# The opening of a fused Mamba-2 and hard-swish kernel: C loaded by heads, and the state ahead of decoding

## The chip, the cores and the metric

The kernel runs on one core of a Trainium2 chip. The core has TensorE (PE in the profile, PEld for its loads of weights), VectorE (DVE), ScalarE (ACT), GpSimd (POOL) and SyncE (SP), which here only issues DMAs. Each engine takes its instructions in the order of the program and waits on semaphores for the others. DMAs are issued from a queue (SP's, or ACT's) and run on sixteen DMA engines. The metric is the time of one execution in microseconds (us); less is better.

## What is computed

The reference, cut to what matters. Inputs: x (4, 8, 768, 32), a (4, 8, 768), B and C (4, 8, 768, 16), w_in (256, 2048), w_out (2048, 256). x, a, B, C are float32, and the two weights come in float64.

```python
# state-space block, chunk by chunk of the sequence; H = 8 heads, N = 16, D = 32
log_a = np.log(np.clip(a, 1e-06, 1.0))
state = np.zeros((batch, H, N, D))
for c in range(nc):
    cum = np.cumsum(la, axis=-1)                       # la: log_a of this chunk
    L = np.exp(cum[..., :, None] - cum[..., None, :]) * causal
    CB = np.einsum('bhin,bhjn->bhij', Cc, Bc)          # "scores"
    y_intra = np.einsum('bhij,bhjd->bhid', CB * L, xc)
    y_inter = np.einsum('bhin,bhnd->bhid', Cc, state) * np.exp(cum)[..., None]
    y[:, :, sl] = y_intra + y_inter
    Bx = Bc (x) xc * np.exp(cum[..., -1:] - cum)
    state = np.exp(np.sum(la, -1)) * state + np.sum(Bx, axis=2)
# then, on y as (3072 tokens, 256):
h = x @ w_in
g = h * np.clip(h + 3.0, 0.0, 6.0) / 6.0
out = g @ w_out
```

## The kernel before

The 768 positions are cut into six chunks of 128, and each chunk c is taken for all four batches at once: 512 tokens. For each chunk the state-space part gives yT (256 features by 512 tokens), and the MLP then runs over 16 blocks f of 128 hidden features. While the MLP of chunk k runs, the state-space part of chunk k+1 is woven into it. The order of all instructions on all engines is written out by hand (a manual schedule): what is called first in the Python code is first in each engine's queue, and there is no planner.

The change lies in the opening: what runs before the first MLP product, from line 1020 to line 1069. It has these parts.

Loads. `a` goes out first on SP's queue; ACT's queue issues the first weights (`load_w(0)`, 1 MB) and B of chunk 0 (line 94, 4096 pieces of 64 bytes); SP's queue then issues C of chunk 0, x of chunk 0 (line 119) and the second weights (`load_w(1)`, line 139). `load_bc` (line 86) has two ways to load. `tokens_first` puts a token in each partition. `pairs_first` (line 97) is used for C of chunk 0 and for B and C of chunks 2 to 5: a partition holds four neighbouring tokens of a head (256 bytes for each batch and parity of the head), with a quarter of the partitions for each pair of heads. It is eight DMAs, one for each batch and each parity of the head, and each covers four heads by 32 rows, so all 128 partitions (line 101).

Decays. log a is summed along the chunk (`add_up`, line 269; a first part for the chunks 0 and 1, the second for the rest), split in three bf16 parts (`in_three`), and PE forms the differences of the sums in PSUM (`diff_less`, `diff_pick`), on top of a mask (`diff_mask`, line 336, and `mask_again`, line 343, which writes the same mask once more in the banks of chunk 0). ACT takes the exponents (`diff_exp`, line 365).

Decoding. The weights come as float64 and are decoded to float32 by a generator, `decode(i)` (line 187), one for each of eight pieces: 0 to 3 are quarters of w_in, 4 to 7 of w_out. Its five steps are taken one by one with `weights(i, n)`. Step 1: ACT copies the top 16 bits (line 198); for piece 0, DVE also forms the significand here (lines 201 and 205). Step 2: DVE masks exponent and sign (215, 217), and for other pieces line 201. Step 3: ACT, line 221. Step 4: ACT, line 223, and for other pieces line 205 on DVE; from piece 1 on it also issues the load of piece i+3, which reuses the buffer of piece i. Step 5: DVE joins exponent and significand (228, 236) in w_in or w_out.

Scores and state. `turn_squares` (line 465) turns C with DVE's 32x32 transposes, `part_heads` (line 475) makes a copy for even and one for odd heads, `fade` (POOL) multiplies the second half by the decays. `turn_b` turns B with PE (line 422), and ACT copies it out of PSUM (line 431). `scores(0)` (line 530) forms C times B, then `into_state` (line 548) the new state's products, which need x. `multiply(0)` (line 579) multiplies the scores by the decays on DVE, `mix(0)` (lines 625 and 503) forms y, `keep(0)` (line 639) copies it to yT on ACT, and `renew(0)` (lines 600 and 558) forms the state for chunk 1 on DVE. `turn_cum` (line 316) turns the sums of chunks 2 to 5, and `by_token` (line 319) negates them into `cum_n`, which is read when chunk 2 is prepared. `busy(n, bank)` (line 493) is n float32 products of the identity that nothing reads.

MLP of chunk 0. `mlp_in` (line 647) multiplies block f; ACT's `ramp` (line 754) and DVE's `times_ramp` (line 759) make g of it. Four PSUM banks take turns, so block f waits for the `times_ramp` of block f-4. Blocks 4i to 4i+3 need quarter i of w_in. The decoding of the pieces 2 to 6 is woven into these blocks, a step for each block. `first_out` (line 772) then multiplies by w_out.

Of the kernel before, what the change touches and what calls it, by code (L numbers as in the profile page):

```python
# [8 lines left out]
FP32 = mybir.dt.float32  # L9
# [5 lines left out]
ALU = mybir.AluOpType  # L15
# [6 lines left out]
def kernel(  # L22
# [24 lines left out]
    nc = tc.nc  # L47
    P = 128
    NB, NH, S, D = x.shape
# [18 lines left out]
    ps = ctx.enter_context(tc.tile_pool(name="ps", bufs=1, space=PSUM))  # L68
# [17 lines left out]
    def load_bc(c):  # L86

        sl = slice(c * P, (c + 1) * P)  # L90

        def tokens_first(src, queue=nc.sync, **where):
            t = loads.tile([P, NB * NH, N], FP32, **where)
            queue.dma_start(out=t, in_=src[:, :, sl, :].rearrange("b h s n -> s (b h) n"))
            return t

        def pairs_first(src):
            t = loads.tile([P, 2, NB, 4, N], FP32, name="pairs", tag="bc")
            for b in range(NB):
                for h in range(2):  # L100
                    nc.sync.dma_start(  # L101
                        out=t[:, h, b].rearrange("s a n -> s (a n)"),
                        in_=src[b, h:NH:2, sl, :].rearrange("h (s a) n -> h s (a n)", a=4))
            return t

        if 0 < c < TURN:
            bcs[c] = [tokens_first(C, name="C", tag="bc")]
        Bs[c] = tokens_first(B, nc.scalar if c == 0 else nc.sync, name="B", bufs=1)
        if c == 0:
            bcs[c] = [pairs_first(C), Bs[c]]  # L110
        elif c < TURN:
            bcs[c].append(Bs[c])
        else:
            bcs[c] = [pairs_first(C), pairs_first(B)]
# [13 lines left out]
    def load_w(i, queue=nc.sync):  # L128

        raw = loads.tile([P, NK * FP * 2 * P], U32, name="raw", bufs=NRAW)  # L130
        if i < NP:
            cols = slice(2 * i * FP * P, 2 * (i + 1) * FP * P)
            src = moe_w_in[:, cols].rearrange("(k p) f -> p k f", p=P)
            dst = raw.rearrange("p (k f) -> p k f", k=NK)
        else:
            r0 = (i - NP) * FP * P
            src = moe_w_out[r0:r0 + FP * P, :].rearrange("(k p) m -> p k m", p=P)
            dst = raw.rearrange("p (k m) -> p k m", k=FP)
        queue.dma_start(out=dst, in_=src)
        raws[i] = raw  # L140
# [14 lines left out]
    def conceal_in(t, pattern):  # L155
# [24 lines left out]
        out=head, in_=head, pattern=[[-2 * N, NQ], [-N, 2]], compare_op=ALU.is_ge,  # L180
        fill=0.0, base=0, channel_multiplier=1)
    nc.gpsimd.affine_select(
        out=head, in_=head, pattern=[[2 * N, NQ], [N, 2]], compare_op=ALU.is_ge,
# [3 lines left out]
    def decode(i):  # L187

        n = NK * FP * P
        top = raws[i].bitcast(U16).rearrange("p (n w) -> p n w", w=4)[:, :, 3]
        lo, hi = (raws[i].rearrange("p (n w) -> p n w", w=2)[:, :, w] for w in range(2))
        s = att.tile([P, n], U16, name="ws")
        e = att.tile([P, n], U16, name="we")
        m = att.tile([P, n], U32, name="wm")
        nc.scalar.copy(out=s, in_=top)

        def significand():  # L200
            nc.vector.tensor_scalar(
                out=m, in0=hi, scalar1=0xFFFFF, scalar2=0x100000,
                op0=ALU.bitwise_and, op1=ALU.bitwise_or)
            yield
            nc.vector.scalar_tensor_tensor(
                out=m.bitcast(FP32), in0=lo, scalar=2.0 ** -32, in1=m, op0=ALU.mult,
                op1=ALU.add)
            yield

        parts_m = significand()  # L210
        if i == 0:
            next(parts_m)
            next(parts_m)
        yield
        nc.vector.tensor_scalar(
            out=e, in0=s, scalar1=0x7FF0, scalar2=None, op0=ALU.bitwise_and)
        nc.vector.tensor_scalar(
            out=s, in0=s, scalar1=0x8000, scalar2=None, op0=ALU.bitwise_and)
        next(parts_m, None)
        yield  # L220
        nc.scalar.activation(e.bitcast(BF16), e, AF.Relu, bias=bias_hi, scale=-8.0)
        yield
        nc.scalar.activation(e, e.bitcast(BF16), AF.Relu, bias=bias_lo, scale=-1.0)
        next(parts_m, None)
        if i and i + NRAW < 2 * NP:
            load_w(i + NRAW)
        yield
        nc.vector.tensor_tensor(out=e, in0=e, in1=s, op=ALU.bitwise_or)
        m, e = m.bitcast(FP32), e.bitcast(BF16)
        if i < NP:  # L230
            dst = w_in[i]
            m, e = (t.rearrange("p (k f) -> p k f", k=NK) for t in (m, e))
        else:
            dst = w_out[:, (i - NP) * FP:(i - NP + 1) * FP, :]
            m, e = (t.rearrange("p (k f) -> p k f", k=FP) for t in (m, e))
        nc.vector.scalar_tensor_tensor(
            out=dst, in0=m, scalar=2.0 ** -20, in1=e, op0=ALU.mult, op1=ALU.mult)
# [35 lines left out]
    def in_three():  # L273
        first = cum[:, :2 * P]
        part = split.rearrange("g c p -> g (c p)")
        nc.vector.tensor_copy(part[:G], first)
        nc.vector.tensor_tensor(out=low, in0=first, in1=part[:G], op=ALU.subtract)
        nc.vector.tensor_copy(mid, low)
        nc.vector.tensor_copy(part[G:2 * G], mid)
        nc.vector.tensor_tensor(out=part[2 * G:pad], in0=low, in1=mid, op=ALU.subtract)  # L280
# [31 lines left out]
    cum_n = const.tile([P, NC, G], FP32, name="cum_n")  # L312
# [3 lines left out]
            nc.tensor.transpose(out=c_ps[:, c], in_=cum_c[:, c], identity=ident[:G, :G])  # L316

    def by_token(c_ps):
        nc.vector.tensor_scalar(
            out=cum_n[:, 2:], in0=c_ps[:, 2:], scalar1=-1.0, scalar2=None, op0=ALU.mult)  # L320


    yTs, states, mids, bTs, bss, tmps = {}, {}, {}, {}, {}, {}
# [17 lines left out]
    def mask_again(c, b):  # L341

        nc.tensor.matmul(
            out=ds[c, b], lhsT=ident_h, rhs=hide.unsqueeze(1).to_broadcast([P, NH, HT]),
            start=True, stop=True)
# [16 lines left out]
    def diff_exp(c, b):  # L362
        if c not in Ls:
            new_decays(c)
        nc.scalar.activation(Ls[c][:, b], ds.pop((c, b)), AF.Exp)
# [25 lines left out]
    def ends(c, b):  # L391

        if b == 0:
            bss[c] = att.tile([P, G, N], FP32, name="bs", bufs=1)
        hs = slice(b * NH, b * NH + NH)
        nc.gpsimd.tensor_tensor(  # L396
            out=bss[c][:, hs], in0=Bs[c][:, hs],
            in1=Ls[c][:, b, :, HT - 1:HT].to_broadcast([P, NH, N]), op=ALU.mult)
# [8 lines left out]
    def turned(c):  # L407
        if c not in bTs:
            bTs[c] = [att.tile([P, NB, P], FP32, name="bT", bufs=1),
                      att.tile([P, NB, 2, P], FP32, name="cT", bufs=1),  # L410
                      att.tile([P, NB, P], FP32, name="csT", bufs=1)]
        return bTs[c]

    def turn_ps(c, j):

        if c < 2:
            return ps.tile([P, NB, P], FP32, name="t_ps", tag=f"f{2 * j if c else 1}")
        return ps_o.tile([P, NB, P], FP32, name="t_ps", tag="o")

    def transposes(c, j, t_ps):  # L420
        for b in range(NB):
            nc.tensor.transpose(
                out=t_ps[:, b],
                in_=bcs[c][j][:, b * NH:(b + 1) * NH].rearrange("s h n -> s (h n)"),
                identity=ident)

    def turn_b(c):

        t_ps = turn_ps(c, 1)
        transposes(c, 1, t_ps)  # L430
        nc.scalar.copy(out=turned(c)[0], in_=t_ps)
# [58 lines left out]
    def busy(n, bank):  # L490

        for _ in range(n):
            nc.tensor.matmul(
                out=bank.rearrange("p (b i) -> p b i", b=NB), lhsT=ident,
                rhs=ident.unsqueeze(1).to_broadcast([P, NB, P]), start=True, stop=True)
# [514 lines left out]
    def weights(i, n):  # L1010
        for _ in range(n):
            next(parts[i], None)


    def diff(c, *bs):
        for part in (diff_less, diff_pick):
            for b in bs:
                part(c, b)
# [6 lines left out]
    row_signs()  # L1025
    add_up(ends_at[0])
    in_three()
    for b in range(3):
        mask_again(0, b)
    diff(0, 0, 1)  # L1030
    diff(0, 2, 3)
# [5 lines left out]
    weights(0, 1)  # L1037
    for b in range(NB):
        ends(0, b)
    turn_b(0)  # L1040
    diff(1, 0, 1)
    weights(0, 1)
    diff_exp(1, 2)
    diff_exp(1, 3)
    turn_squares(bcs[0][0], turned(0)[2])
# [3 lines left out]
    store_rows()  # L1049
    load_w(2)  # L1050
    weights(0, 1)
    busy(2, ps.tile([P, NB * P], FP32, name="d", tag="f3"))
    scores(0)
    multiply(0)
    load_w(3)
    c_ps = ps.tile([P, NC, G], FP32, name="c_ps", tag="f1")
    turn_cum(c_ps)
    busy(1, ps.tile([P, NB * P], FP32, name="d", tag="f0"))
    weights(0, 1)
    weights(1, 1)  # L1060
    by_token(c_ps)
    mix(0)
    keep(0)
    weights(1, 3)
    renew(0)
    weights(1, 1)
    load_eto(1)
    load_bc(1)
    load_x(1)
# [175 lines left out]
```

## Time and profile before

| | us |
|---|---|
| three runs | 339.91, 339.91, 340.11 |
| median | 339.91 |
| the profiled execution | 339.78 |
| its span, from the first to the last instruction | 337.6 |

| engine | busy, us | share of the span |
|---|---|---|
| PE | 330.6 | 98% |
| DVE | 234.5 | 69% |
| ACT | 199.4 | 59% |
| POOL | 123.9 | 37% |

The profile is that of one execution. Times in it count from the start of the span. L101 is line 101 of the kernel before. "SPq" is SP's queue of DMA issues; a row "out<-in" names the tiles that an instruction writes and reads. In the view of waits, "A <- B" says that A's engine sat idle until B ended. In the chain of waits, each piece is followed back from the last instruction to what released it. A timeline's row has the start, the time from the first start to the last end, the engine, line, operation, tiles and shapes, the count, and in brackets the idle time ahead and what ended it. A float32 product of PE shows as two records.

### The profile page before, as it was taken

The numbers are of one execution on the slowest core, as the hardware profiler recorded it, in microseconds if no ns is written. First come the engines' busy times: TensorE is split into PE (matmuls) and PEld (weight loads), VectorE is DVE, ScalarE is ACT, GpSimd is POOL, SyncE is SP. The second block draws the span as 40 slices with busy tenths as digits, with TensorE's granted clock in tenths as the row PEclk, the third lists the DMA queues.
The fourth block names the chain that finished last, engine by engine and source line by source line (L and its number), as shares of the span: only waits on it lengthen the run. The fifth ranks groups of instructions, "written<-read, shape, count | busy, mean of one in ns | idle before, by whom it ended". The sixth has DMA issues, their size and how long they took to land.

```text
span 337.6 us, 8192 instructions
## 1 busy us (share of the span) xinstructions
PE 330.6 (98%) x3337; PEld 265.4 (79%) x3337; DVE 234.5 (69%) x380; ACT 199.4 (59%) x418; POOL 123.9 (37%) x123
## 2 busy tenths in 40 slices
PE   6999999999999999999999999999999999999996
PEld 2554448888888888888888888888888888899995
DVE  6699999998399739755339556355477355599974
ACT  4769878757986670576461576570486030577661
POOL 3300000290184799089813079911079800000000
PEclk9999999999999999999999999999999999999999
DMA  8999968042590215258107267101160001110001
GB/s 174 165 316 201 208 219 184 2 54 76 139 142 1 57 37 139 33 72 78 33 13 156 33 83 69 28 4 17 27 81 2 2 2 18 26 21 2 1 2 62
DMA packets 89605, 25.15 MB, mean 75 GB/s; under 512 B 82208, under 2 KB 85952, under 8 KB 89056
## 3 DMA queue, kind: packets, MB, share of 16 engines
q1 hardware_dynamic: 85184, 23.33, 37.5%
q10 hardware_dynamic: 4384, 1.31, 1.8%
q8 instruction: 26, 0.43, 0.5%
q14 instruction: 11, 0.09, 0.1%
HBM read 21.33 MB, written 3.29 MB: 73 GB/s over the span
## 4 chain that ended last, share of the span: by engine, by line
PE 94%; DMA 3%; DVE 1%; SPq 1%; issue 0%; DVEq 0%
PE h L715 33%; PE wb L914 13%; PE wc L914 8%; PE o L772 8%; PE h L647 8%; PE wa L914 8%; PE o_end L880 6%; PE y L625 3%; PE y L503 2%; PE cb L530 2%; DMA raw<-in_moe_w_in_dram 2%; DMA pairs<-in_C_dram 1%; PE y L548 1%; SPq L101 1%; PE o_end L898 1%; PE sp L548 0%
## 5 line engine op out<-in xcount | busy, mean ns | idle before, releaser
L759 DVE SCALAR_TENSOR_TENSOR gT<-gT,h 128x512 f32<-128x512 f32 x96 | 64.8, 684 | 33.8 <-ACT gT L754 32.2
L754 ACT ACTIVATE gT<-h,half 128x512 f32<-128x512 f32 x96 | 65.2, 685 | 25.6 <-PE h L715 23.6
L735 ACT ACTIVATE h<-h 128x512 f32<-128x512 f32 x66 | 38.2, 585 | 39.0 <-PE h L715 38.8
L715 PE MATMUL h<-y_hi,w_part 128*128 128x512 f32 x160 | 51.5, 407 | 0.0
L715 PE MATMUL h<-y_less,w_part 128*128 128x512 f32 x160 | 50.1, 399 | 0.0
L715 PE MATMUL h<-y_lo,w_part 128*128 128x512 f32 x160 | 49.5, 395 | 0.0
L818 POOL TENSOR_TENSOR s<-gT 128x512 f32<-128x512 f32 x16 | 23.8, 1490 | 46.7 <-DVE gT L759 46.7
L715 PEld LDWEIGHTS h<-y_lo,w_part 128*128 128x128 f32 x160 | 30.0, 188 | 7.3
L715 PEld LDWEIGHTS h<-y_hi,w_part 128*128 128x128 f32 x160 | 30.0, 188 | 6.8 <-DVE gT L759 0.2
L715 PEld LDWEIGHTS h<-y_less,w_part 128*128 128x128 f32 x160 | 29.2, 188 | 6.0 <-ACT h L735 0.2
L385 ACT ACTIVATE L<-L,cum_n 128x64 f32<-128x64 f32 x128 | 31.6, 336 | 0.0
L772 PE MATMUL o<-w_out,gT 128*128 128x256 f32 x128 | 28.8, 381 | 0.0
L647 PE MATMUL h<-yT,w_in 128*128 128x512 f32 x64 | 27.7, 594 | 0.0
L772 PEld LDWEIGHTS o<-w_out,gT 128*128 128x128 f32 x128 | 24.1, 190 | 3.8 <-issue 0.5
L647 PEld LDWEIGHTS h<-yT,w_in 128*128 128x128 f32 x64 | 12.1, 190 | 14.9 <-issue 13.2
L158 POOL TENSOR_SCALAR_AFFINE_SELECT L<-L 64x1024 f32<-64x1024 f32 (+1 forms) x16 | 20.4, 1281 | 8.5 <-DMA L<-cum_d 8.0
L579 DVE TENSOR_TENSOR L<-L,cb 128x512 f32<-128x512 f32 x24 | 15.0, 681 | 11.7 <-PE cb L530 11.7
L403 POOL TENSOR_TENSOR tmp<-state,eto 128x256 f32<-128x256 f32 x5 | 3.2, 643 | 52.8 <-ACT eto L389 48.9
L818 POOL TENSOR_TENSOR s<-gT,s 128x512 f32<-128x512 f32 x16 | 21.7, 1364 | 0.9
L396 POOL TENSOR_TENSOR bs<-B,L 128x128 f32<-128x128 f32 x24 | 11.2, 486 | 29.5 <-ACT L L385 20.9
L880 PE MATMUL o_end<-v_pair,g_pair 128*128 128x256 f32 x120 | 21.1, 281 | 0.0
L818 POOL TENSOR_TENSOR gT<-gT 128x512 f32<-128x512 f32 x16 | 20.4, 1279 | 0.9
(140 smaller groups left out, 593.0 us busy)
## 6 DMA issues: line engine op xcount, KB each, us to landing
raw<-in_moe_w_out_dram SPq DMA_DIRECT2D x4, 1024.0 KB
L<-cum_d SPq DMA_DIRECT2D x8, 512.0 KB
xt<-in_x_dram SPq DMA_DIRECT2D x6, 512.0 KB
raw<-in_moe_w_in_dram SPq DMA_DIRECT2D x3, 1024.0 KB
out_dram<-back SPq DMA_DIRECT2D x128, 16.0 KB
pairs<-in_C_dram SPq DMA_DIRECT2D x40, 32.0 KB
eto<-cum_e SPq DMA_DIRECT2D x20, 64.0 KB
B<-in_B_dram SPq DMA_DIRECT2D x5, 256.0 KB
```

The lines of the kernel that those rows point to most:

```text
L158: nc.gpsimd.affine_select(out=t[rows], in_=t[rows], pattern=pattern, compare_op=ALU.is_ge, fill=-1e5, base=base, channel_multiplier=-1)
L385: nc.scalar.activation(Ls[c][:, b, h], Ls[c][:, b, h], AF.Exp, bias=cum_n[:, c, g:g + 1])
L579: nc.vector.tensor_tensor(out=Ls[c][:, :, hs], in0=Ls[c][:, :, hs], in1=cbs[c][q], op=ALU.mult)
L647: nc.tensor.matmul(out=h, lhsT=w_in[f // FP][:, j, f % FP * P:(f % FP + 1) * P], rhs=yTs[k][:, j].rearrange("p b i -> p (b i)"), start=(j ...
L715: nc.tensor.matmul(out=hs_[k, f], lhsT=w[j][:, f % FP * P:(f % FP + 1) * P], rhs=y[:, j], start=(start and j == 0), stop=True, skip_group_ ...
L735: nc.scalar.activation(h, h, AF.Copy, scale=1.0 / EPS + 1.0)
L754: nc.scalar.activation(gTs[k][:, f], h, AF.Relu, bias=half, scale=1.0 / 6.0)
L759: nc.vector.scalar_tensor_tensor(out=g, in0=g, scalar=1.0, in1=h, op0=ALU.min, op1=ALU.mult)
L772: nc.tensor.matmul(out=o[:, b % 2], lhsT=gTs[0][:, f, b * P:(b + 1) * P], rhs=w_out[:, f], start=(f == 0 and b % 2 == 0), stop=True, skip_ ...
L818: nc.gpsimd.tensor_tensor(out=o, in0=p_, in1=q_, op=op)
L880: nc.tensor.matmul(out=ends_["cross" if n == 2 else "squares"][b], lhsT=g_parts[t][n][:, b * P:(b + 1) * P], rhs=w, start=(t == 0 and b < ...
L914: nc.tensor.matmul(out=bank[:, slot], lhsT=lhs[:, j], rhs=rhs[:, j], start=(clear and j == 0), stop=True, skip_group_check=True)
```

## The change

- `pairs_first` still issues eight DMAs of 32 KB, but one for each head in place of one for each batch and parity. Each now covers 32 partitions, with the four batches inside, and in both patterns the 32 rows stand outermost (before, the pattern of the source had the four heads outermost). What lies in the tile is the same. It holds for all uses of `pairs_first`.
- `mask_again` runs for all four batches in place of three.
- Piece 0's third decoding step (ACT, line 221) stands ahead of `turn_b` in place of behind it.
- The two idle products ahead of `scores(0)` are dropped; the one behind `turn_cum` stays.
- `by_token` goes from DVE to ACT and stands ahead of piece 0's last step.
- Piece 1's decoding, whose steps lay ahead of `mix(0)`, behind `keep(0)` and behind `renew(0)`, is now one run of five steps behind `renew(0)`. In `decode`, piece 1 forms the first half of its significand (line 201) in step 1, so line 205 comes in step 2.

```diff
         def pairs_first(src):
             t = loads.tile([P, 2, NB, 4, N], FP32, name="pairs", tag="bc")
-            for b in range(NB):
-                for h in range(2):
-                    nc.sync.dma_start(
-                        out=t[:, h, b].rearrange("s a n -> s (a n)"),
-                        in_=src[b, h:NH:2, sl, :].rearrange("h (s a) n -> h s (a n)", a=4))
+            for h in range(NH):
+                rows = slice(h // 2 * 32, h // 2 * 32 + 32)
+                nc.sync.dma_start(
+                    out=t[rows, h % 2].rearrange("s b a n -> s b (a n)"),
+                    in_=src[:, h, sl, :].rearrange("b (s a) n -> s b (a n)", a=4))
             return t
...
         parts_m = significand()
-        if i == 0:
-            next(parts_m)
+        for _ in range(2 - i):
             next(parts_m)
...
     def by_token(c_ps):
-        nc.vector.tensor_scalar(
-            out=cum_n[:, 2:], in0=c_ps[:, 2:], scalar1=-1.0, scalar2=None, op0=ALU.mult)
+        nc.scalar.mul(cum_n[:, 2:], c_ps[:, 2:], -1.0)
...
-    for b in range(3):
+    for b in range(NB):
         mask_again(0, b)
...
     for b in range(NB):
         ends(0, b)
+    weights(0, 1)
     turn_b(0)
     diff(1, 0, 1)
-    weights(0, 1)
     diff_exp(1, 2)
     diff_exp(1, 3)
...
     weights(0, 1)
-    busy(2, ps.tile([P, NB * P], FP32, name="d", tag="f3"))
     scores(0)
     multiply(0)
     load_w(3)
     c_ps = ps.tile([P, NC, G], FP32, name="c_ps", tag="f1")
     turn_cum(c_ps)
     busy(1, ps.tile([P, NB * P], FP32, name="d", tag="f0"))
+    by_token(c_ps)
     weights(0, 1)
-    weights(1, 1)
-    by_token(c_ps)
     mix(0)
     keep(0)
-    weights(1, 3)
     renew(0)
-    weights(1, 1)
+    weights(1, 5)
     load_eto(1)
     load_bc(1)
     load_x(1)
```

## The prediction

> **What bounds the kernel now.** I read the page's head first, to see whether any engine leaves room.
>
> ```profile
> span 337.6 us, 8192 instructions
> PE 330.6 (98%) x3337; PEld 265.4 (79%) x3337; DVE 234.5 (69%) x380; ACT 199.4 (59%) x418; POOL 123.9 (37%) x123
> ```
>
> PE is busy for 98% of the span, so time can only be won where the work that ends last is not PE's. That is in the opening, and the chain of waits (start, length, what) shows where:
>
> ```profile
> 0.80 5.94 DMA raw<-in_moe_w_in_dram
> 6.76 0.57 SPq L101
> 7.38 1.49 SPq L101
> 8.91 4.00 DMA pairs<-in_C_dram
> 13.09 1.17 DVE csT L465
> 14.28 0.89 DVE cT L475 x2
> 15.30 1.25 PE cb L530 x59
> ...
> 22.60 27.66 PE h L647 x64
> 50.27 9.93 PE o L772 x46
> ```
>
> From 16.5 us on it is nearly all PE; up to 15.3 us it is the loads of C, two copies of C on DVE, and the scores. Third, who waited (us in all, times, longest), and busy time by stretch: the stretch, its sum, then PE, PEld, DVE, ACT, POOL with counts, granted clock, DMA's mean share and GB/s.
>
> ```profile
> DVE csT L465 <- DMA pairs<-in_C_dram: 2.9, 1, 2.9
> POOL bs L396 <- DMA B<-in_B_dram: 5.4, 1, 5.4
> SPq L101 <- DMA raw<-in_moe_w_in_dram: 0.2, 1, 0.2
> ...
> 4.00:6.00 2.00, 2.00 (x6) 0.66 (x5) 1.96 (x6) 1.08 (x3) 1.01 (x1) 1.00 1.06 371
> 8.00:10.00 2.00, 2.00 (x72) 1.46 (x72) 1.93 (x4) 1.41 (x3) 0.00 (x0) 1.00 0.39 47
> ```
>
> While C is what all wait for, DMA moves 47 GB/s; just before it moved 371. The trace's landing marks say why: each of the eight loads of C gets four marks when its data lands, a 32-row store of L935 gets sixteen. So C runs on four of the sixteen DMA engines, 256 packets of 256 B on each. Last, the timelines, for what stands next to the wait:
>
> ```profile
> 9.80 0.43 DVE L217 TENSOR_SCALAR ws<-ws 128x1024 uint16<-128x1024 uint16 x1
> 12.89 1.98 PE L493 MATMUL d<-ident 128*128 128x512 f32 x4
> 18.75 1.15 ACT L198 COPY ws<-raw 128x1024 uint16<-128x1024 uint16 x1 [0.53 <-DMA raw<-in_moe_w_in_dram]
> 22.65 0.37 ACT L639 COPY yT<-y 128x256 f32<-128x256 f32 x1 [0.26 <-PE y L503]
> 27.15 1.28 DVE L759 SCALAR_TENSOR_TENSOR gT<-gT,h 128x512 f32<-128x512 f32 x2
> 48.12 1.23 DVE L236 SCALAR_TENSOR_TENSOR w_out<-wm,we 128x1024 f32<-128x1024 f32 x1
> ```
>
> DVE is free for C at 10.23 and gets it at 13.09. PE ends its real work at 12.89 and fills with idle products. And DVE's backlog after the opening reaches to 49.35, close to PE's first product with w_out near 50.1: that will matter.
>
> **Loads of C.** Still eight issues of 32 KB, 1024 packets of 256 B, but each over 32 rows. SP's eight issues ran from 1.26 to 9.54; the fifth and seventh were long (2.33, 1.49), as I read it because four engines had to drain first, and the sixth was held at 6.76 by the landing of the first weights. That hold stays: sixth 6.76, seventh 7.38, eighth 8.0. From issue to landing I have two bounds: 1.5 us (a 32-row store of L935) and 3.1 us (a load of C in a quiet stretch, 72 to 75 us, on four engines). C is whole at 9.5 to 11.1 instead of 12.91; I take 10.2, nearer the store, since its shape is the new one. By a rule of the Trainium skill (DMA: Bandwidth & Descriptors, "How many engines (k)") 32 rows outermost run on all sixteen; no load of this trace shows that. B, on the same engines, lands before 11.15. For C and B of later chunks the same edit costs nothing: their loads end near 83 us and DVE turns them at 107.7.
>
> **From C to the scores.** Three strands meet at L530. DVE: free at 10.23, then 1.16 (csT) and 0.88 (cT x2), so 12.3; if C came at 11.1, 13.2. PE: the work that ended at 12.89 had waited 0.11 for B, so 12.8; the two idle products (1.98) are gone, which would else have ended at 14.8. ACT: L221 (1.15) now comes ahead of the copy bT (0.59); from 11.04, where the copy of eto ends, that is 12.7. Scores start at 12.85 where they started at 15.30: 2.45 earlier, bounds 2.1 (late C) and 2.5. The fourth repeat of the mask costs one product at the spacing of its neighbours, 0.43; PE idled 0.52 there for split. Without that cover it would cost 0.43.
>
> **From the scores to the first MLP product.** 15.30 to 22.53, 7.23 us, moves as a block if two things hold. x must be there for L548: x landed 6.05 after its issue, twelve of its sixteen parts 5.2 to 5.6 after; issued at 8.6, that is 13.8 to 14.7. L548 would start at 14.0 and has 0.61 of slack (PE then waits for DVE), so this costs 0 to 0.1. And the f32 product busy(1) stays. The negated copy of c_ps, 0.28 on DVE, goes to ACT, which idles 0.52 ahead of the copies yT: nothing on the path, and 0.3 if that gap were gone. MLP starts at 20.08.
>
> **Decoding the second quarter of w_in.** This part loses. Before, ACT's first step (L198) ran at 18.75, in a gap; now it stands behind the copies yT, which end 0.49 after the MLP's start. From there all is serial: L198 1.15, L215 0.42, L221 1.15, L223 1.15, L228 0.69, L236 1.14 to where the next may start, and some 0.06 of hand-overs net. DVE's first L759 comes 6.25 after the MLP's start, at 26.33; before it came 4.62 after, at 27.15. So PE is 2.45 earlier and DVE only 0.82: a lag of 1.63. The new state (1.07 on DVE) and L201 now lie in DVE's wait for L198 and cost nothing. load_w(4), issued in the fourth step, waits as before for L205 (23.75 by the same sum), so SP's loads queued behind it (eto, C, B, x of chunk 1) don't move; the earliest user is past 60 us. load_w(2), behind store_rows and so behind the second scan, goes out some 2.7 earlier. No edit moves anything past POOL's work, whose order stays.
>
> **Does DVE make the lag good?** From 27.15 to 49.26 it is busy for 21.0 of 22.1 us, and its rest is waits for ACT in the same interleaving. I see nothing to win. Then PE meets DVE: w_in's last quarter is ready at 42.34 and first used near 43.24 (0.90 to spare); w_out's first at 49.35, used at 50.10 (0.76 to spare). The smaller decides: PE can use 0.82 + 0.76 - 0.03 of hand-over = 1.55 of its 2.45. Later DVE waits for PE again (0.59 at 73.56, and the next product that needs it is 1.4 after), so nothing more is lost.
>
> **Sum.** 2.45 won ahead of the MLP, 0.90 given back in it: 1.55. The profiled execution took 339.78 (span 337.6 and 2.2 around it), 0.13 under the median of three, 339.91. 339.78 - 1.55 = 338.23, and with the 0.13, 338.4.
>
> **Rivals.** (1) The lag is absorbed: ACT and DVE interleave better once PE is ahead. Then all 2.45 stay: 337.5. Against it: DVE's 1.1 us of rest in 22. (2) The reverse: a wait lands in the decode chain, say the second weights, which landed at 18.73 and are now needed at 20.5. They go out 1.2 earlier, so it needs a jam of 3; each us beyond goes through whole. A delay of 1.0 to 1.5 gives 339.4 to 339.9. (3) Slower: the loads of C don't get faster, because all sixteen engines also carry 4096 packets of B at that time and the sixth issue is held anyway. If C lands at 12.9 the MLP starts at 22.53 as before, DVE's lag of 1.63 meets 0.76 of slack, and the kernel loses 0.9: 340.8. The point from which it decides is a gain of 0.9 at the scores, that is C at 12.0. Against it: B's parts on engines that it had to itself landed by 9.3 us; 64 packets of C more on each, at some 15 ns as after 10 us, add 1.0. (4) PE falls to half rate without its idle products. The masks up to 7 us were spaced 0.43, the same shape (L348) 0.22 afterwards, so two rates exist here, though the granted clock shows 1.00 for both. Were the stretch from the scores to the MLP's second block at half rate, mix (3.2), busy(1) and two blocks would take up to 3 us more, the gain at the MLP would be gone and the lag would stay: 340.8. Against it: PE's longest gap by my walk is 0.6 us, and before, after 3.4 us of small products, busy(1) still ran at its fast spacing. The Trainium skill (TensorE: Matmul & The Clock Gate, Part 1) puts the fall after about 3.4 us of idling, which by this walk would not happen; by that rule the sum stands unless C is late.
>
> **How the numbers follow.** Forecast 0.58, its own range 338.0 to 338.9 (the bounds at the scores give 338.3 to 338.7, x 0.1, and runs differ by 0.2); rival 1 0.11; rival 2 0.13; rival 3 0.11; rival 4 0.05; 0.02 left for anything else slower. A change under 0.2% (0.68 us) can't be told from none here. Faster: 0.58, 0.11 and a small part of rival 2, 0.71; same: most of rival 2, 0.12; slower: 0.17. The range runs from 337.3, rival 1 with the upper bound at the scores (337.4) less half the spread of the runs, to 340.3, which takes in rival 2 and leaves 3 and 4 out.
>
> **What would show it.** Right: sixteen landing marks per load of C; C whole by 10 to 11 us; DVE with no wait ahead of csT; L530 at 12.8 to 13.0; the first L647 near 20.1 and the first L759 near 26.3; PE waiting some 0.9 us in all within L647 or ahead of the first L772, for DVE. Wrong: csT still waiting for C past 12 us, L198 waiting for its weights, matmul spacing of 0.43 for L348's shape after 12 us, or no PE wait in the MLP.

## The result, and the profile after

| | median, us | runs | lowest and highest |
|---|---|---|---|
| before | 340.13 | 17 | 339.64, 342.23 |
| after | 343.44 | 17 | 340.33, 346.44 |

The change makes the kernel slower: the ratio is 1.0068, 95% interval 1.0044 to 1.0092, and the medians differ by 3.3 us, where 1.5 us less had been forecast. Ratios here and below leave out slow executions, over 1.5% above the fastest of their kernel: of the change these are five (345.87 to 346.44), and without them its median is 342.4. The executions of the changed kernel lie widely apart, from 340.33 to 346.44; the section on e12 reads that spread. The profiled one took 344.55 (span 342.4, 2.15 around it), 1.1 above the median; that of before 339.78 (span 337.6).

The head of the page and its row of the granted clock in 40 slices, after. PE has as much work as before (330.5 us), its share of a longer span is smaller, and two slices near the start have a clock below full speed, where before had a 9 everywhere.

```profile
span 342.4 us, 8188 instructions
PE 330.5 (97%) x3334; PEld 266.0 (78%) x3334; DVE 234.3 (68%) x379; ACT 199.0 (58%) x419; POOL 124.0 (36%) x123
...
PEclk9987999999999999999999999999999999999999
```

The chain of waits of after (start, length, what):

```profile
7.72 0.43 SPq L101
8.15 0.04 issue
8.20 7.85 DMA xt<-in_x_dram
16.05 0.14 issue
16.18 1.05 PE y L546 x54
...
18.64 0.87 PE y L623 x52
19.51 3.35 issue
22.86 0.42 PE y L623 x4
...
26.49 29.01 PE h L645 x64
55.49 6.69 PE o L770 x31
```

Lines are 1 or 2 lower than in the kernel before: L528 is the scores, L546 the products that need x, L623 and L501 are mix, L645 the MLP. Three things are to be seen. C and its turn on DVE have left the chain: what is waited for is x. Mix starts at 18.64, 0.75 earlier than before (19.39, in the line below). Then PE stands still for 3.35 us in the middle of mix, put down to "issue", which means that it waited for nothing that the profile shows. The chain of before, at the same place:

```profile
19.39 1.00 PE y L625 x57
20.38 0.61 PE y L503 x16
```

The timeline of PE around that stop (start, length, engine, line, operation, in brackets the idle time ahead) shows that it cuts one row of 64 equal products after the sixtieth. The four that follow have the same tiles and shapes, so I take it that no data were missing. Behind it the products are slower: L501's sixteen take 1.11, where they took 0.68 before.

```profile
18.57 0.94 PE L623 MATMUL y<-L,xt 64*32 64x64 f32 x60
22.86 0.42 PE L623 MATMUL y<-L,xt 64*32 64x64 f32 x4 [3.35 <-issue]
23.21 1.11 PE L501 MATMUL y<-csT,mid 32*64 32x64 f32 x16
```

Busy time by stretch (PE, PEld, DVE, ACT, POOL with counts, then granted clock, DMA share, GB/s), after:

```profile
20.00:22.00 2.00, 0.00 (x0) 0.00 (x0) 1.26 (x4) 0.00 (x0) 0.00 (x0) 1.00 1.03 410
22.00:24.00 2.00, 1.14 (x18) 0.98 (x20) 0.00 (x0) 0.37 (x1) 0.00 (x0) 0.58 0.64 256
24.00:26.00 2.00, 2.00 (x84) 1.71 (x82) 0.00 (x0) 0.74 (x2) 0.00 (x0) 0.50 0.03 10
28.00:30.00 2.00, 2.00 (x4) 0.73 (x3) 1.93 (x3) 1.56 (x2) 0.00 (x0) 0.71 0.00 0
```

In 20 to 22 us no product runs while the DMA engines are full. Then the clock is halved: reckoned from the shares of 0.5 us stretches (0.83 in 22.0 to 22.5, 0.85 in 29.0 to 29.5) from 22.33 to 29.15. That gives the whole account up to the first product with w_out, 50.27 before and 55.49 after: mix 0.75 earlier; the stop 3.35; mix without the stop 4.50 instead of 3.21, so 1.29 more at half clock; the MLP's 64 products 29.00 instead of 27.67, 1.33 more, which is half of the 2.66 us that it ran at half clock. Sum 5.22. The span is 4.8 longer, so 0.4 came back later; where, I did not follow.

**What PE waits for.** The page's list of DMA queues has one that no line of the kernel issues (packets, MB, share):

```profile
q8 instruction: 26, 0.43, 0.5%
```

These are 26 packets of 16 KB. PE has some 6,700 instructions in the trace (products, loads of weights, semaphores), and 26 times 256 is 6,656; I read it as PE's own program, 256 instructions a packet, and the places of the stops bear that out. Counted through the trace from 0, the stop sits ahead of PE's instruction 705, and other experiments stop at 449, 1985, 4033, 5057 and 6081, all 193 plus a multiple of 256. In the stretch 20.3 to 21.5 us the packet that PE waits for is seen among the weights (queues, packets, MB, share):

```profile
q1 hardware_dynamic: 127, 0.47, 96.9%
q8 instruction: 1, 0.02, 5.7%
```

It ran from 20.35 to 21.45, and PE went on at 22.86. In the kernel before, the same packet ran from 17.84 to 18.84, and PE came to the same instruction at 20.07, 1.23 after the packet's end. In the runs below where PE stood, it went on 1.2 to 1.5 us behind the packet's end: the kernel before was already at the edge, and nothing in its chain showed it.

Why does the packet begin late? No row shows when it is asked for, or on which DMA engine it runs. I read it as a place in line: PE would ask for the block when it enters the one before, at instruction 449, which is at 16.38. The loads of the weights of quarters 2 and 3 (one row of SP's queue, first in the change, then before) were issued at 15.97, ahead of that, and at 16.53, 0.15 behind it; in the kernel before at 17.17 and 17.75, both behind its 449 (16.21).

```profile
15.97 0.99 SPq L139 DMA_DIRECT2D raw<-in_moe_w_in_dram  x2
17.17 2.05 SPq L139 DMA_DIRECT2D raw<-in_moe_w_in_dram  x2
```

The page "Runtime: NRT & Kernel Launch" of the Trainium skill, section "Instruction fetch mechanics", describes blocks of 256 instructions that each engine's sequencer fetches by a DMA queue of its own while it runs the block before; with that these runs agree. It calls the cost mostly hidden; here it is 3.35 us in one place, and the measurement decides.

### The profile page after: what moved, and what is told of

Read it like the earlier page. It is cut to its first block, busy times and chain, and to the rows that moved or that the text cites. A ratio compares the mean times of both kernels' runs of the same rounds, so it can differ in the third digit from the quotient of the medians.

```text
span 342.4 us, 8188 instructions
## 1 busy us (share of the span) xinstructions
PE 330.5 (97%) x3334; PEld 266.0 (78%) x3334; DVE 234.3 (68%) x379; ACT 199.0 (58%) x419; POOL 124.0 (36%) x123
## 3 DMA queue, kind: packets, MB, share of 16 engines
HBM read 21.33 MB, written 3.29 MB: 72 GB/s over the span
## 4 chain that ended last, share of the span: by engine, by line
PE 93%; DMA 4%; issue 1%; SPq 0%; DVE 0%
PE h L713 33%; PE wb L912 12%; PE h L645 8%; PE wc L912 8%; PE o L770 8%; PE wa L912 8%; PE o_end L878 6%; PE y L623 3%; PE y L501 2%; DMA xt<-in_x_dram 2%; DMA raw<-in_moe_w_in_dram 2%; PE cb L528 2%; PE y L546 1%; PE o_end L896 1%; PE sp L546 0%
## 5 line engine op out<-in xcount | busy, mean ns | idle before, releaser
L757 DVE SCALAR_TENSOR_TENSOR gT<-gT,h 128x512 f32<-128x512 f32 x96 | 64.8, 684 | 33.8 <-ACT gT L752 32.2
L645 PE MATMUL h<-yT,w_in 128*128 128x512 f32 x64 | 29.1, 616 | 0.0
L645 PEld LDWEIGHTS h<-yT,w_in 128*128 128x128 f32 x64 | 12.6, 199 | 15.8 <-issue 13.9
L158 POOL TENSOR_SCALAR_AFFINE_SELECT L<-L 64x1024 f32<-64x1024 f32 (+1 forms) x16 | 20.3, 1275 | 8.8 <-DMA L<-cum_d 8.3
L816 POOL TENSOR_TENSOR gT<-gT 128x512 f32<-128x512 f32 x16 | 20.3, 1277 | 0.9
```

Of the source, the lines that this page charges most:

```text
L158: nc.gpsimd.affine_select(out=t[rows], in_=t[rows], pattern=pattern, compare_op=ALU.is_ge, fill=-1e5, base=base, channel_multiplier=-1)
L645: nc.tensor.matmul(out=h, lhsT=w_in[f // FP][:, j, f % FP * P:(f % FP + 1) * P], rhs=yTs[k][:, j].rearrange("p b i -> p (b i)"), start=(j ...
L757: nc.vector.scalar_tensor_tensor(out=g, in0=g, scalar=1.0, in1=h, op0=ALU.min, op1=ALU.mult)
L816: nc.gpsimd.tensor_tensor(out=o, in0=p_, in1=q_, op=op)
```

## The experiments

Four theories stood at one time or another. F: the program's packets queue behind loads that now go out earlier. D: the new order of decoding and state costs the time. K: the two idle products that are gone cost it, by PE's clock. P: it is only where the blocks' borders fall in the work. Each kernel below computes the whole output. Each ratio is against executions of the kernel before in the same round, whose medians were 340.49 (e1 to e8), 340.46 (e9, e10) and 340.34 (e11, e12).

The rows that the verdicts share, from the traces of the profiled executions (us; "block 1" and "block 2" are the first two packets of that queue, needed at PE's instructions 449 and 705; "w2" is the issue of the weights of quarter 2):

| kernel | block 1 | 449 at | w2 | block 2 | 705 at | stop there | median |
|---|---|---|---|---|---|---|---|
| before | 10.70-11.83 | 16.21 | 17.17 | 17.84-18.84 | 20.07 | 0 | 340.13 |
| after | 13.47-15.00 | 16.38 | 15.97 | 20.35-21.45 | 22.86 | 3.35 | 343.44 |
| e1 | 13.52-15.03 | 16.41 | 15.92 | 20.58-21.57 | 22.98 | 3.21 | 340.43 |
| e2 | 10.94-12.06 | 16.43 | 17.16 | 18.25-19.26 | 20.51 | 0.28 | 341.52 |
| e3 | 13.59-15.09 | 16.55 | 18.33 | 17.73-18.89 | 21.10 | 0 | 340.25 |
| e4 | 13.44-14.96 | 16.30 | 15.93 | 21.33-22.30 | 23.69 | 1.40 | 358.25 |
| e5 | 13.34-14.87 | 16.17 | 16.31 | 17.74-19.59 | 21.00 | 1.70 | 342.52 |
| e6 | 13.10-14.63 | 15.87 | 17.87 | 17.34-18.59 | 19.97 | 0 | 340.21 |
| e7 | 10.88-11.98 | 15.91 | 17.16 | 19.08-20.03 | 21.38 | 2.35 | 343.50 |
| e8 | 10.88-12.27 | 16.02 | 17.27 | 19.12-20.08 | 21.49 | 2.35 | 342.81 |
| e9 | 13.46-14.96 | 16.29 | 18.02 | 17.60-18.93 | 20.39 | 0.53 | 339.38 |
| e10 | 11.71-13.21 | 15.22 | 17.16 | 17.92-19.02 | 20.25 | 1.25 | 339.67 |
| e11 | 11.41-12.41 | 16.38 | 14.67 | 20.10-21.11 | 22.45 | 2.07 | 344.43 |
| e12 | 13.55-15.05 | 16.43 | 15.86 | 20.57-21.58 | 23.00 | 3.16 | 343.90 |

### e1: the loads of C by heads, alone

```diff
-            for b in range(NB):
-                for h in range(2):
...
+            for h in range(NH):
+                rows = slice(h // 2 * 32, h // 2 * 32 + 32)
...
```

> The kernel before with the loads of C by heads alone; the order of the rest, the two idle products and the decoding stay. In the trace of the change PE stands still for 3.35 us inside mix (19.51 to 22.86), with nothing named as the cause, and a 16 KB packet of kind 'instruction' lands in that gap (20.35 to 21.45). Theory F (PE waits for its own program: the block is asked for when PE passes the start of L548's products and queues behind the weight loads that SP has issued by then): here C lands near 11.8 as in the change, the second scan ends near 15, so load_w(2) goes out near 16 and again ahead of that block; a stop of 2 to 4 us inside mix, some 342 to 345. Theory D (the loss lies in the new order of decoding, as the forecast's lag did): none here, so the earlier C shows as a gain limited by the idle products (they end at 14.8): 339.3 to 339.9. Theory K (without the idle products PE falls to half rate): no loss here either, same time as D.

340.43 (339.55 to 345.75, 10 runs), ratio 1.0018 (0.9987 to 1.0050): no difference that can be told. But the profiled execution took 344.58, and it has the stop:

```profile
19.77 3.21 issue
22.98 0.43 PE y L625 x6
```

So the stop needs neither the new order nor the missing idle products: earlier loads of C are enough, in part of the executions.

### e2: everything but the loads of C

The edit puts the old loop over `b` and parity back in the changed kernel.

> The change without its loads of C: C by batches on four engines as before, everything else as in the change. Theory F: C lands near 12.9, the second scan ends near 16.3 and load_w(2) goes out near 17.2, behind PE's request for its block, so no long stop in mix; the lag of the decoding costs what the forecast gave for late C, 0.9: 340.5 to 341.2. Theory D: the loss stays whole, 343 or more. Theory K: PE idles 2.4 us ahead of the scores, more than in the change, so half rate from there and 343 or more.

341.52 (340.78 to 344.83, 10 runs), ratio 1.0047 (1.0023 to 1.0071). The stop is 0.28 only, and the loss sits elsewhere. Chain of waits:

```profile
22.87 0.37 ACT yT L637
23.25 1.02 ACT ws L198
...
28.98 1.28 DVE gT L757 x2
...
42.94 1.24 DVE w_in L235
44.18 0.04 issue
44.22 7.13 PE h L645 x16
```

From 23.25 to 44.18 it runs through ACT's and DVE's steps of decoding, where the chain of before has one row of PE. DVE's first L757 comes 6.22 after the first MLP product (22.76), where it came 4.62 after it before; and PE's last sixteen products of the MLP wait for DVE, which writes w_in's last quarter until 44.18. The product ahead of them starts at 43.27 and its neighbours are 0.43 apart, so they were due at 43.70 and start 0.52 late, at 44.22.

```profile
22.76 21.10 PE L645 MATMUL h<-yT,w_in 128*128 128x512 f32 x48
44.22 7.13 PE L645 MATMUL h<-yT,w_in 128*128 128x512 f32 x16 [0.36 <-DVE w_in L235]
```

All 64 products take 28.60 (22.76 to 51.36), where they took 27.74 before (22.53 to 50.27; from the start of the first product's own row, 0.07 ahead of its piece in the chain). D is real: 0.86 us in this trace, 1.0 by the medians of the round (341.52 against 340.49). It can't be all of the 3.3 us of the change, and e2 has no long stop.

### e3: the change with the weights of quarters 2 and 3 issued later

```diff
     store_rows()
-    load_w(2)
...
     multiply(0)
-    load_w(3)
...
     by_token(c_ps)
+    load_w(2, nc.scalar)
+    load_w(3, nc.scalar)
     weights(0, 1)
```

> The change with load_w(2) and load_w(3) issued from ACT's queue right behind by_token (near 18.3) in place of SP's queue at 15.97 and 16.53; nothing else moves. Theory F: the block of the program no longer has these two loads ahead of it, so its packet starts near 18 as before (17.84) and the stop in mix shrinks from 3.35 to under 1 us; first MLP product near 22 to 23, time 339.5 to 341. Theories D and K: nothing changes, a loss of 3 us as in the change.

340.25 (339.93 to 343.83, 10 runs), ratio 1.0008 (0.9985 to 1.0031): the 3.3 us are back, with the new order and without the idle products. Block 2 starts at 17.73 and the stop at 705 is gone. The two stores of L285 and L287, which the change also moved ahead of instruction 449 (15.11 and 15.49; before, 16.31 and 16.69, behind it), are still ahead of it in e3 (15.03 and 15.40), so they are not what holds the packet. The profiled execution is the slowest of the ten, and it shows the next wall: PE reaches instruction 449 1.10 us before it can go on, since block 1 ended at 15.09 only (11.83 in the kernel before), and by 16.07 the clock is halved, until 29.72.

```profile
15.45 1.10 issue
16.55 1.17 PE y L546 x59
17.72 0.56 PE c_ps L315 x4
18.28 2.01 PE d L491 x2
```

The two products of L491 take 2.01 us; at full clock they take 1.05 (the change, at 17.59).

### e4: the change with 40 tiny products ahead of the scores

```diff
     weights(0, 1)
+    small(40, ps.tile([P, NB * P], FP32, name="d", tag="f3"))
     scores(0)
```

`small` is n products of 128 by 32 that nothing reads. They take 1.2 us and move every later border by 80 instructions.

> The change with 40 tiny extra products (32x32, bf16, read by nobody) in PE's idle time ahead of the scores, 80 instructions for about 1 us of a gap of 1.4. Theory F: all borders between 16 KB blocks of PE's program move 80 instructions forward, so the border now at the start of L548 falls into L530, PE asks for the block near 14.6 and ahead of load_w(2); the stop comes earlier in mix and is under 1.5 us or gone; 339 to 342. Theory D: no change from 343. Theory K: the extra products keep PE busier ahead of the scores, a part of the loss may go, but the matmul spacing and not the stop would show it.

358.25 (356.11 to 360.31, 4 runs), ratio 1.0525 (1.0464 to 1.0586), 15 us above the change, which I had not foreseen. The stops are at the same instruction numbers, which are now other products; the timeline of PE:

```profile
14.06 0.72 PE L534 MATMUL cb<-cT,bT 32*64 32x128 f32 x26
16.30 1.55 PE L534 MATMUL cb<-cT,bT 32*64 32x128 f32 x38 [1.51 <-issue]
...
21.53 0.76 PE L629 MATMUL y<-L,xt 64*32 64x64 f32 x20
23.69 0.94 PE L629 MATMUL y<-L,xt 64*32 64x64 f32 x44 [1.40 <-issue]
```

Instruction 449 now falls in the scores and 705 after 20 products of mix, not 60. New stops come at 1985, 4033, 5057 and 6081 (1.5 to 2.1 us each, by the starts on both sides), where dense rows of small products lie. So the stop goes with the count of instructions, not with a product or its operands. Where the borders fall seems worth several us, but P alone is no remedy; the 15 us also hold the products' own 1.2 us and more half clock (mean 0.971 against 0.990 in the profiled executions), and I did not separate them.

### e5: quarters 1 to 3 loaded as four DMAs of 256 KB each

```diff
-        queue.dma_start(out=dst, in_=src)
+        if 0 < i < NP:
+            n4 = FP * P // 2
+            for j in range(4):
+                queue.dma_start(out=dst[:, :, j * n4:(j + 1) * n4], in_=src[:, :, j * n4:(j + 1) * n4])
```

> The change with each 1 MB load of w_in's quarters 1 to 3 issued as four DMAs of 256 KB, at the same place in SP's order. A block of PE's program came after the first three 1 MB loads had drained in the change (20.35). If a block waits only for the DMA that its engine is at (theory F1, turn by turn between queues), it now waits for a quarter of one, about 0.6 us: packet near 17.5, no long stop in mix, 340 to 341.5. If it waits for everything that SP's queue had handed over before it (theory F2, first come first served), the stop stays near 3 us and the time at 342 to 346.

342.52 (341.77 to 343.03, 4 runs), ratio 1.0056 (1.0041 to 1.0070). The packet starts at 17.74, 2.6 earlier than in the change; but it takes 1.85 (1.10 in the change), and the stop is 1.70. This does not decide between the two forms of the theory: with more issues on SP's queue the first load of quarter 2 went out at 16.31, behind PE's instruction 449 (16.17) and no longer ahead of it, so order and length changed together. In e3, where no load of quarter 2 or 3 is issued before 18.33, the packet starts at the same time (17.73). Whether the length of a transfer ahead counts is not shown. The clock is halved here too, from 21.85 to 28.68.

### e6: e3 with the two idle products back

```diff
     weights(0, 1)
+    busy(2, ps.tile([P, NB * P], FP32, name="d", tag="f3"))
     scores(0)
```

> e3_w_late (loads of quarters 2 and 3 late) with the two idle products put back ahead of the scores. In e3's trace the product behind turn_cum (L491) took 2.01 us where before took 1.12, so PE was at half rate from about 16.5 on and the MLP took 30.2 in place of 27.7. Theory K2 (without the idle products PE falls to half rate in this stretch): L491 back at 1.1, the MLP near 28, and the time 0.5 to 1.5 below e3 in those executions where it fell. Theory F alone (the stop in front of L546, which waits for a block of the program, 15.23 to 16.55, causes it): the stop is still there, less the time that the idle products fill; no gain over e3, 340.0 to 340.6.

340.21 (339.57 to 340.85, 10 runs), ratio 0.9988 (0.9978 to 0.9997). The median is that of e3, but the two executions of e3 near 342 and 344 have no like here. PE comes to instruction 449 at 15.87 without a stop: block 1 ended at 14.63, and the idle products had kept PE from being ready before (in e3 it was ready at 15.45, and block 1 ended at 15.09). No stretch has half the clock in the profiled execution: K is right as far as that.

### e7 and e8: x and quarter 1 issued later too, with the new and with the old order of decoding

```diff
+    load_x(0, nc.scalar)
     first_eto()
...
     turn_b(0)
+    load_w(1, nc.scalar)
```

Both start from e3 (no idle products). e8 has also the old order of decoding and state.

> e3_w_late with the loads of x and of quarter 1 also taken from SP's queue and issued from ACT's: x behind the four exponents of chunk 0 (near 10.7), quarter 1 behind the copy bT (near 12.5). In the change x went out at 8.20 (9.59 before) and the first block's packet came at 13.47 (10.70 before). Theory F: with no load of x ahead of it the first block's packet is back near 10.7, the second comes near 16.5, no stop over 0.3 us from the scores to the MLP; the MLP starts near 21.2, and the lag of the decoding takes 0.9 of that: 339.2 to 340.0. If other traffic (C, B) delays the first block, it stays after 12.5 and the time at e3's 340.2 or above.

> e7_late_all with the decoding of quarter 1 where the kernel before had it (ACT's first step ahead of mix, the rest ahead of the new state), so without the lag that the forecast priced at 0.9. If fetch and lag are the two losses and C by heads the one gain, this is the sum: 338.3 to 339.2, under the kernel before. If the lag is not worth 0.9: no gain over e7.

e7 343.50 (343.28 to 344.29, 4 runs), ratio 1.0090 (1.0076 to 1.0104); e8 342.81 (340.26 to 344.45, 10 runs), ratio 1.0057 (1.0023 to 1.0091). That was to be a gain and is a loss. Block 1 is early again (10.88 in both), as F has it. But quarter 1, issued at 12.1 instead of 8.7, now lies ahead of block 2, which starts at 19.08 and 19.12 although the weights of quarter 2 go out behind PE's instruction 449. The wall was moved from one block to the next.

### e9: e6 with the old order of decoding

```diff
     load_w(2, nc.scalar)
-    load_w(3, nc.scalar)
     weights(0, 1)
+    weights(1, 1)
+    load_w(3, nc.scalar)
     mix(0)
     keep(0)
+    weights(1, 3)
     renew(0)
-    weights(1, 5)
+    weights(1, 1)
```

> e6_late_busy (C by heads, quarters 2 and 3 late, both idle products) with the decoding of quarter 1 where the kernel before had it. In e6 PE still waits 0.95 in the MLP (42.73 to 43.68) for DVE's decoding of the last quarter of w_in, as the forecast's lag said. Theory: that wait goes, and with it 0.7 to 1.0: 339.2 to 339.5, about 1 under the kernel before. If the lag isn't it: 340.2 as e6. If the stop in mix comes back because ACT's step for quarter 1 moves the late loads: above 341.

339.38 (338.61 to 339.71, 6 runs), ratio 0.9969 (0.9957 to 0.9981): faster than both kernels, by some 1 us. It is the kernel before with C by heads, `by_token` on ACT ahead of mix, the fourth mask, piece 0's third step ahead of `turn_b`, and the weights of quarters 2 and 3 issued from ACT behind it. Against e6 the order is worth 0.83, close to what the MLP took longer in e6 than before (28.59 against 27.74; the expectation's 0.95 runs from one start to the next and holds a product's own 0.43). Its chain still has a stop at instruction 705, and the MLP starts where it did before:

```profile
19.04 0.83 PE y L624 x50
19.87 0.53 issue
...
22.72 27.66 PE h L646 x64
50.38 11.65 PE o L771 x54
```

What it wins, it wins behind that: at 50.38 it is 0.11 later than the profiled execution before, and its span ends 0.5 earlier (337.1). Which later row brings this, I did not find out.

### e10: e9 with x and quarter 1 in four DMAs each, and one idle product

> e9_late_w with the load of x in four DMAs (one for each batch), that of quarter 1 in four, and one idle product in place of two ahead of the scores. e5_split showed that a block of PE's program gets in between DMAs of SP's queue. Theory F1: the first block's packet comes near 11 to 12 in place of 13.1, the second near 16 to 17; no stop; x whole near 15.5, L548's products start 0.4 earlier than in e9; 0.3 to 0.8 under e9: 338.5 to 339.2. Against: more DMAs on SP (six more at 0.43) hold back its later ones, or one idle product is too little and PE falls to half rate: at or above e9's time.

339.67 (338.91 to 343.07, 12 runs), ratio 0.9989 (0.9965 to 1.0013). The scores start at 14.09 and mix at 18.17, 1.2 earlier than before. Block 2 gives all of it back:

```profile
18.17 0.83 PE y L635 x50
19.00 1.25 issue
...
22.57 27.66 PE h L657 x64
```

The MLP starts at 22.57 where it started at 22.60. PE is at instruction 449 at 15.22, but the packet of block 2 still starts at 17.92 only, so this opening can't use an earlier C.

### e11: the kernel before, with two loads moved up

```diff
+    load_w(2)
+    load_w(3)
     store_rows()
-    load_w(2)
...
-    load_w(3)
```

> The kernel before, with one thing changed: the loads of the second and third MLP weights stand ahead of the stores of by_token in SP's program, so that SP issues them as soon as it has issued quarter 1 (about 13.9) and not behind by_token (17.2). Theory F (PE's program comes in blocks of 256 instructions over the same DMA engines, and a block asked for behind a large load waits for it): PE asks for the block that it needs at record 705 only when it enters the one before, at about 16; the loads are then ahead of it, its packet ends 1.5 to 2.5 us later than the 18.84 of before, PE stops for 1.5 to 3.5 us in mix, and the time is 342 to 345 us. Theory D (the order of the decode steps is what costs the time) and theory K (the two idle products that are gone cost it, by PE's half rate): both are as in the kernel before, so the time stays at 340.1, or falls by the 0.9 us of the second weights.

344.43 (343.41 to 344.99, 4 runs), ratio 1.0107 (1.0071 to 1.0142). Nothing of the change is in this kernel: C is loaded the old way, the scores start at 15.47, the order of decoding is the old one, the idle products are there. Only two loads go out 2.5 us earlier, at 14.67 and 15.27, and the whole loss is there:

```profile
15.47 1.25 PE cb L530 x59
...
19.55 0.83 PE y L625 x50
20.38 2.07 issue
...
25.82 29.62 PE h L647 x64
```

With e3, which takes the early loads out of the change and gets the time back, this settles the cause: the early loads delay the packet, PE stops, and half clock follows (here from 22.90 to 29.73). The detail of F, how the packet waits its turn among the transfers, stays a reading.

### e12: the change with the two idle products back

The edit is that of e6, on the changed kernel.

> The change with the two idle products alone put back ahead of the scores. Theory K (PE at half rate for want of them is the loss): the time goes back to 340 us, without the long first MLP products. Theory F: the stop at record 705 in mix stays at 2 to 3.5 us in the profiled execution, because the blocks come as late as before; PE falls to half rate behind the stop, and the time is 341 to 345 us.

343.90 (340.42 to 346.39, 10 runs), ratio 1.0059 (1.0022 to 1.0097). K falls as the first cause: the stop is 3.16, and half clock follows it from 22.9 to 29.7.

This run and the change show how the spread arises. Half clock comes in pieces of one length: 22.33 to 29.15 in the change, 21.85 to 28.68 in e5 (6.82 to 6.83 each), 16.07 to 29.72 in e3 (13.65), all multiples of 3.41. One such piece takes 0.005 off an execution's mean granted clock. Sorted by that clock, the seventeen executions of the change are: at 0.999 and over, 340.33 and 340.82; at 0.995, five from 341.40 to 343.44; at 0.990, five from 341.80 to 345.20; at 0.983 to 0.985, five from 345.87 to 346.44. All six of e9 are at 0.998 and over. I take the long times to be executions with a stop long enough to halve the clock; only the profiled ones show the stop itself.

## Why the prediction was wrong

**Loads of C: the mechanism right, the size not.** Each load has sixteen landing marks, and SP's issues ended at 8.15. C was whole at 11.75, not 10.2, past the bound of 11.1; before it was 12.91. The last three loads landed 4.0 to 4.1 after their issue. The forecast's 1.5 is near for the same loads at 81 us (1.8), but at 8 to 10 us the engines were busy (DMA share 1.56, against 0.39 before). The sixteen engines that C now uses also carried B, as rival 3 had it; I take that as the reason, and no run tests it. So csT still waited for C, 1.75 instead of 2.86, and the scores came at 14.11, 1.19 earlier and not 2.45.

**"From the scores to the first MLP product ... 7.23 us, moves as a block": this step failed.** It made the time depend on x and on one idle product. x came at 16.05, past the bound of 14.7: fifteen of its parts were there by 14.55, and the last came 1.50 later. Block 1 took 1.53, from 13.47 to 15.00, so I take that part to have shared its DMA engine. (The bound rests on x's last landing before, 6.05 after its issue; of the sixteen parts eleven, not twelve, lay within 5.2 to 5.6.) And the step left out PE's program. Block 1 ended at 15.00 instead of 11.83, behind x and C that had been issued earlier (in e7, which issues x and quarter 1 later, it starts at 10.88 again). With the 1.2 to 1.5 us that PE took after a packet, it could not pass instruction 449 before 16.2, whatever x did; block 2 then cost 3.35. The first product of the MLP started at 26.42, where the forecast had 20.08.

**"load_w(2) ... goes out some 2.7 earlier" was costed at nothing.** It went out 1.2 earlier, and that is the term of the sum that is missing: e11, which moves quarters 2 and 3 by 2.5, prices it at 4.1 us on the kernel before (344.43 against 340.34, its median beside e11), e3 at 3.2 in the change (343.44 against 340.25, medians of different rounds).

**Decoding the second quarter: right.** The first L757 was forecast 6.25 after the MLP's start; it came 6.22 after it in e2 and 6.21 in the change (32.63 and 26.42). The 0.90 that the MLP was to give back was 0.86 in e2. In the profiled change the wait is not seen, since PE at half clock needs its weights later.

**Rivals.** None was the cause. Rival 3 (C no faster) is half true: the gain at the scores was 1.19, and its point of decision was 0.9. Rival 4 saw the half clock, but took it for a consequence of the missing idle products; it follows a stop for instructions, and e12 and e11 have it with the idle products in place. Only in e3 against e6 do these products matter, at the border at 449. What the Trainium skill says (TensorE: Matmul & The Clock Gate, Part 1) of a window of about 3.4 us agrees with the pieces of 3.41 us. But it was applied to the gaps of a walk that had no stop in it, and half clock came behind a stop of 1.70 us in e5, and in e3 within one of 1.10 us.

**What could have been seen.** The trace of before had it all: 26 packets of an instruction queue on the page, one of them at 17.84 to 18.84 just behind the issue of the weights of quarters 2 and 3 (17.17 and 17.75), and 1.23 us between its end and the product that needed it.

## What to carry to other kernels

In these runs an engine's program was a load like any other. Where a stretch has hundreds of small instructions on one engine, look up when the packets of its instruction queue land and what was issued ahead of them, before any large load is moved up into that stretch. A stop put down to "issue" in the middle of equal products, at a multiple of 256 instructions from the last such place, was this in every run here. Loads that nobody needed soon were better issued behind the place where PE would ask for its block (e3, e9), and a gain ahead of such a wall was worth nothing until the packet came earlier too (e10).

## What the runs showed of the hardware that I had not expected

- PE went on 1.2 to 1.5 us after the packet with its next instructions had ended (1.41 in the change, 1.34 in e11, 1.25 in e2).
- The packet's own time varied: block 2 took 1.00 before, 1.10 in the change, and 1.85 in e5, among loads cut in four. Why is not shown.
- With 80 more small instructions, which shift the borders, four further stops came, and the kernel took 15 us more than 343 (e4).
- The granted clock was halved for 6.82 us after a stop of 1.70 us (e5) and around one of 3.35 us (the change), for 3.41 after one of 2.35 us (e8), and not after one of 1.25 us (e10). But in e3 it was halved for 13.65 us, from 16.07 on, within a stop of 1.10 us, so the length of the stop alone does not decide. In e5 it fell when PE had been running again for 0.85 us.
